# New cost numbers for the list scheduler of a fused attention and two-MLP kernel

## The chip, the core and the metric

One core of a Trainium2 chip runs the whole program. The metric is the device time of one launch in microseconds (us). Engines are named as the profile names them: PE (TensorE matmul) and PEld (its weight load), DVE (VectorE), ACT (ScalarE), POOL (GpSimd) and SP (SyncE, which issues all the DMAs here). Each engine works through its own instruction stream strictly in order; an instruction whose inputs are not there holds up everything behind it on that engine.

## What is computed

```
scores = 0.125 * q @ k^T                      # 4 batches x 8 heads, 576 x 576, head size 64
keep the scores >= the row's 32nd largest      # top_k = 32
a = softmax of the kept ones;  x = a @ v       # x becomes [2304, 512]
h = x @ w_in;  x = (h * cos(h)) @ w_out        # 512 -> 2048 -> 512
P = exp(x @ w_gate), normalised 8 times over rows and columns    # [2304, 8]
out = sum over e of P[:, e] * (relu(x @ w1[e]) @ w2[e])          # 8 experts, 512 -> 1024 -> 512
```

w_in and w_out arrive as 64-bit floats, as pairs of 32-bit words.

## The kernel before

Rows of x are handled in tiles of 128 tokens. An *attention tile* (`att_tile`, L436) is 128 queries of one head against all 576 keys; there are 144 of them. On DVE such a tile is a MAX8 (L459), three rounds of MATCH_REPLACE8 (L464) and MAX8 (L465) that find the 32nd largest score, a mask that multiplies and sums (L466), and a reciprocal (L469). Around these stand score products on PE (L447 and L448, or L451 for the first tiles), copies and exp on ACT (L457, L461), small steps and the normalisation on POOL (L460, L468, L470), transposes on PE (L475), the split of the transposed tile into a high and a low part (L493 on ACT, L494 on DVE) and the products with v (L501, L503).

Nearly all large products are made of three fp32r products of high and low parts (`mm3`, L370). A weight is loaded by DMA into `raw`, ACT copies it to a high part (L345), and POOL or DVE subtracts for the low part (L347).

The program has these stages, which overlap:

- **Head.** The first three attention tiles of all eight heads (`attention_tile`, 24 of the 144 tiles) are done in plain fp32. Beside them `decode` (L315) turns 32 chunks of w_in and w_out into fp32: a DMA of 0.5 MB, a bit operation on DVE (L325), four ACT steps (L326 to L329), a POOL product (L330), a second bit operation on DVE (L331), two more POOL steps (L332, L333) and a store to DRAM. For each of the three tiles follows the first MLP: `moe1_tile_a` (products L629, the cosine gate with L588 and L589 on POOL, L590 and L595 on DVE, transposes L638) and `moe1_tile_b` (products L654, transposes L661, and the split L668/L669 into `x2fh` and `x2fl`). The third L669 completes x2f for the first 384 tokens.
- **Fills.** From then on PE has `fill(e, 0, 3)` (L762) for all eight experts: expert products for these 384 tokens, which need nothing but weights. They stand beside the rest of attention of batch 0 and all of batch 1. Their gates are L758 on ACT and L759 on DVE.
- **The first wide MLP part** (`moe1`, 512 tokens) needs batch 1's attention to be done; its second products are L383, L384 and L387. It yields x2f for four more tiles, whose fills (`fill(e, 3, 4)`) stand beside the attention of batches 2 and 3.
- **Three more MLP parts, the normalisation of P** (`sinkhorn`), and then 32 rounds over the experts for the remaining tokens.

The code writes none of the order by hand. Every instruction is given to a `Plan` with an engine, an estimated cost in ns, what it reads and writes, and a priority by engine and class of work (`PRIORITY`, L28: on PE the first attention goes first, then the first MLP, then attention, then the rest; on DVE the MLP goes first, then decode, then first attention, then attention). `Plan.issue` plays the engines forward in its own estimated time: it takes the engine that is free earliest, lets it take the ready operation of best priority, and adds the estimated cost and a latency. The order in which operations are taken is the order of the emitted program. So an estimate changes no instruction, only the place at which it stands in its engine's stream. Ring buffers (four raw chunks in decode, two `wk`, four score tiles) turn into dependencies in the same way. Inside a plan DMAs share one rate, and a plan counts a PE product double where it takes PE's clock to be low.

Of the kernel before, what the change touches and what calls it, by code (L numbers as in the profile page):

```python
# [12 lines left out]
I32 = mybir.dt.int32  # L13
U32 = mybir.dt.uint32
AF = mybir.ActivationFunctionType
ALU = mybir.AluOpType
# [7 lines left out]
LOWEST = -3.0e38  # L24
# [46 lines left out]
class Plan:  # L71
# [78 lines left out]
    def issue(self):  # L150
# [15 lines left out]
        while len(order) < len(ops):  # L166
            best = None
            for e in engines:
                if now[e]:
                    t = free[e]  # L170
                elif soon[e]:
                    t = max(free[e], soon[e][0][0])
                else:
                    continue
                if best is None or t < best[0]:
                    best = (t, e)
            t, e = best
            while soon[e] and soon[e][0][0] <= t:
                k = heapq.heappop(soon[e])[1]
                heapq.heappush(now[e], (ops[k].prio, k))  # L180
            k = heapq.heappop(now[e])[1]
            op = ops[k]
            cost = op.cost
            if op.func and op.func != func:
                cost, func = cost + 1283.0, op.func
            if e == "PE":
                w = int(t / 3413)
                if w != window:
                    past = busy.get(w - 1, 0.0) / 3413
                    warm = past > 0.95 or (warm and past > 0.5)  # L190
                    window = w
                cost *= 1.0 if warm else 2.0
                a = t
                while a < t + cost:
                    z = min(t + cost, (int(a / 3413) + 1) * 3413.0)
                    busy[int(a / 3413)] = busy.get(int(a / 3413), 0.0) + z - a
                    a = z
            free[e] = op.end = t + cost
            if e == "SP":
                dma_free = max(t + cost + 650.0, dma_free) + op.bytes / 360.0  # L200
                op.end = dma_free + 900.0
            order.append(k)
            for o in op.outs:
                n = ops[o]
                n.ready = max(n.ready, op.end + self.LAT.get((e, n.eng), 130.0))
                n.left -= 1
                if not n.left:
                    heapq.heappush(soon[n.eng], (n.ready, o))
# [3 lines left out]


def mm_ns(n):
    return max(107.0, n / 2.4 + 3.0)


def act_ns(n, psum=False, ap=False):
# [11 lines left out]
def fused_kernel(tc, kq, vv, w_in, w_out, w_gate, w1, w2, out, B=4):  # L230
# [31 lines left out]
    def put(eng, cost, emit, reads=(), writes=(), func=None, nbytes=0):  # L262
        return add(eng, cost, emit, reads, writes, PRIORITY[eng][CLASSES.index(work)], func, nbytes)
# [51 lines left out]
    def decode(src, keep, part):  # L315

        raw, mag, sgn, low = d_raw(), d_mag(), d_sgn(), d_low()  # L320
        dma(lambda: raw.ap, lambda: src.bitcast(I32), 1 << 19, writes=[raw])
        hi = lambda dt: raw.ap.bitcast(dt).rearrange("p (n t) -> p n t", t=2)[:, :, 1]
        lo = lambda: raw.ap.bitcast(U32).rearrange("p (n t) -> p n t", t=2)[:, :, 0]
        magf = lambda: mag.ap.bitcast(F32)
        put("DVE", 335, lambda: V.tensor_scalar(mag.ap, hi(I32), 3, 0x40000000, op0=ALU.logical_shift_left, op1=ALU.bitwise_xor), [raw], [mag])  # L325
        put("ACT", 613, lambda: A_.activation(sgn.ap, hi(F32), AF.Identity, bias=cols.ap[:, 1:2]), [raw, cols], [sgn])  # L326
        put("ACT", 613, lambda: A_.activation(sgn.ap, sgn.ap, AF.Sign, bias=cols.ap[:, 2:3]), [sgn, cols], [sgn])
        put("ACT", 520, lambda: A_.activation(low.ap, lo(), AF.Copy, scale=2.0**-52), [raw], [low])
        put("ACT", 520, lambda: A_.activation(magf(), magf(), AF.Abs), [mag], [mag])  # L329
        put("POOL", 1225, lambda: G_.tensor_tensor(magf(), magf(), sgn.ap, op=ALU.mult), [mag, sgn], [mag])  # L330
        put("DVE", 335, lambda: V.tensor_scalar(sgn.ap.bitcast(I32), mag.ap, -8388608, None, op0=ALU.bitwise_and), [mag], [sgn])  # L331
        put("POOL", 1225, lambda: G_.tensor_tensor(low.ap, low.ap, sgn.ap, op=ALU.mult), [low, sgn], [low])  # L332
        put("POOL", 1225, lambda: G_.tensor_tensor(low.ap, magf(), low.ap, op=ALU.add), [mag, low], [low])  # L333
        dma(keep, lambda: low.ap, 1 << 18, [low], [part])
# [101 lines left out]
    def att_tile(stats, dests, plain=None):  # L436
# [24 lines left out]
        put("ACT", act_ns(S, ap=True), lambda: A_.activation(ex.ap, sc.ap, AF.Exp, scale=0.125, bias=mc(32)), [sc, (m, 32, 33)], [ex], func="exp")  # L461
        for r in range(3):
            src = wk if r else sc
            put("DVE", 669, lambda r=r, src=src: V.match_replace(wk.ap, mc(8 * r, 8), src.ap, LOWEST), [src, (m, 8 * r, 8 * r + 8)], [wk])  # L464
            put("DVE", 669, lambda r=r: V.max(mc(8 * r + 8, 8), wk.ap), [wk], [(m, 8 * r + 8, 8 * r + 16)])  # L465
        put("DVE", 729, lambda: V.scalar_tensor_tensor(ex.ap, sc.ap, mc(31), ex.ap, op0=ALU.is_ge, op1=ALU.mult, accum_out=mc(33)),  # L466
            [sc, ex, (m, 24, 32)], [ex, (m, 33, 34)])
        put("POOL", 162, lambda: G_.tensor_scalar(mc(34), mc(33), 1e-9, 1.0, op0=ALU.add, op1=ALU.mult), [(m, 33, 34)], [(m, 34, 35)])  # L468
        put("DVE", 75, lambda: V.reciprocal(mc(35), mc(34)), [(m, 34, 35)], [(m, 35, 36)])  # L469
# [624 lines left out]
```

## Time and profile before

| what | value |
|---|---|
| three runs, us | 2480.79, 2482.40, 2483.55; median 2482.4 |
| the profiled execution, us | 2480.47; span 2478.7 |
| PE busy | 2364.7 us, 95% |
| DVE busy | 1986.9 us, 80% |
| ACT, POOL busy | 1271.7 us and 1266.6 us, 51% each |
| chain that ended last, by engine | PE 57%, DVE 28%, POOL 6% |
| DMA | 261.37 MB, mean 105 GB/s, 263 GB/s in the busiest of 40 slices |

Busy means that an instruction of the engine was under way; a matmul is pipelined and its end modelled, so that matmuls that start 0.227 us apart are each 0.39 us long and overlap. The chain of waits follows the last instruction back to what released each step. Both PE and DVE stand high, so the stages have to be read apart, which the rows further down do.

### The profile page before, as it was taken

The page shows a single profiled execution, that of the slowest core. Times are in us where ns is not written, and L with a number is a line of the kernel's source. Part 1 is how long each engine was busy: PE and PEld are TensorE (multiplying, and loading weights), DVE is VectorE, ACT ScalarE, POOL GpSimd, SP SyncE. Part 2 cuts the span into 40 slices and gives each one's busy share as a digit, 9 for nine tenths or more (in the row PEclk, how much of TensorE's full clock was granted, in tenths as well). Part 3 has the DMA queues.
Part 4 walks back from the last instruction along what each step waited for, and adds up shares of the span by engine and source line. Part 5 has one row for each costly group of instructions (what it writes and reads, how often), then busy time and mean ns, then how long its engine had stood idle before and what let it go on. Part 6 is the DMA issues. An engine that isn't in the chain of part 4 may idle for free.

```text
span 2478.7 us, 33516 instructions
## 1 busy us (share of the span) xinstructions
PE 2364.7 (95%) x11089; PEld 1905.7 (77%) x11089; DVE 1986.9 (80%) x3651; ACT 1271.7 (51%) x2438; POOL 1266.6 (51%) x1328
## 2 busy tenths in 40 slices
PE   6878999999889999999999999999999999999999
PEld 3434688888667877778878888788888888888887
DVE  8997599999998999999986787776666666666655
ACT  6785566666578666666566776322322222322221
POOL 6886487767577656656520033433443334443330
PEclk9889999999899999999999999999999999999999
DMA  8765654444323333333334333022222221111101
GB/s 263 232 210 186 200 167 144 139 123 151 109 74 97 114 115 115 115 119 97 97 114 123 91 108 104 27 64 81 81 85 81 73 60 35 36 42 43 35 22 47
DMA packets 159501, 261.37 MB, mean 105 GB/s; under 512 B 15008, under 2 KB 60656, under 8 KB 159328
## 3 DMA queue, kind: packets, MB, share of 16 engines
q1 hardware_dynamic: 159328, 259.24, 34.5%
q8 instruction: 87, 1.43, 0.2%
q14 instruction: 86, 0.70, 0.1%
HBM read 227.31 MB, written 31.87 MB: 105 GB/s over the span
## 4 chain that ended last, share of the span: by engine, by line
PE 57%; DVE 28%; POOL 6%; issue 4%; ACT 3%; DMA 1%; SPq 0%; POOLq 0%; ACTq 0%; DVEq 0%
PE y L372 9%; PE y L373 9%; PE y L374 9%; DVE wk L464 7%; DVE m L465 6%; DVE ex L466 4%; PE g L374 2%; PE g L373 2%; PE g L372 2%; DVE m L459 2%; POOL wlo L347 2%; DVE atl L494 1%; PE y L383 1%; PE y L387 1%; PE y L384 1%
## 5 line engine op out<-in xcount | busy, mean ns | idle before, releaser
L347 POOL TENSOR_TENSOR wlo<-raw,whi 128x512 fp32r<-128x512 f32 x336 | 451.7, 1349 | 195.1 <-ACT whi L345 116.3
L465 DVE MAX8 m<-wk 128x8 f32<-128x576 f32 x432 | 318.1, 748 | 1.9
L953 DVE SCALAR_TENSOR_TENSOR acc<-y,P,acc 128x512 f32<-128x512 f32 x308 | 229.2, 748 | 103.5 <-PE y L374 103.2
L345 ACT ACTIVATE whi<-raw 128x512 fp32r<-128x512 f32 x416 | 259.2, 627 | 96.5 <-PE y L374 36.9
L464 DVE MATCH_REPLACE8 wk<-m,wk 128x576 f32<-128x576 f32 x288 | 213.5, 742 | 1.1
L372 PE MATMUL y<-whi,gh 128*128 128x512 f32 x448 | 182.0, 406 | 0.0
L372 PE MATMUL y<-gh,xh 128*128 128x512 f32 x450 | 177.1, 393 | 1.0 <-DVE acc L949 1.0
L374 PE MATMUL y<-whi,gl 128*128 128x512 f32 x448 | 176.5, 394 | 0.0
L373 PE MATMUL y<-gl,xh 128*128 128x512 f32 x450 | 176.5, 392 | 0.0
L374 PE MATMUL y<-gh,xl 128*128 128x512 f32 x450 | 176.2, 392 | 0.0
L373 PE MATMUL y<-wlo,gh 128*128 128x512 f32 x448 | 176.0, 393 | 0.0
L475 PE MATMUL t<-ident,ex 128*128 128x128 f32 (+1 forms) x720 | 136.6, 290 | 39.7 <-POOL ex L470 10.9
L457 ACT ACTIVATE sc<-s 128x288 f32<-128x288 f32 x288 | 117.0, 406 | 95.6 <-DVE ex L466 54.9
L475 PEld LDWEIGHTS t<-ident,ex 128*128 128x128 f32 (+1 forms) x720 | 85.9, 140 | 101.6 <-POOL ex L470 27.8
L466 DVE SCALAR_TENSOR_TENSOR ex<-sc,m,ex 128x576 f32<-128x576 f32 x144 | 152.8, 1061 | 3.6 <-ACT ex L461 1.8
L470 POOL TENSOR_SCALAR ex<-ex,m 128x576 f32<-128x576 f32 x144 | 111.2, 772 | 33.9 <-DVE m L469 33.0
L493 ACT ACTIVATE ath<-t 64x128 fp32r<-64x128 f32 (+3 forms) x272 | 104.5, 396 | 46.2 <-PE t L475 40.0
L461 ACT ACTIVATE ex<-sc,m 128x576 f32<-128x576 f32 x144 | 111.3, 773 | 32.4 <-POOL m L460 31.4
L459 DVE MAX8 m<-sc 128x8 f32<-128x576 f32 x144 | 106.9, 743 | 9.2 <-ACT sc L457 9.1
L464 DVE MATCH_REPLACE8 wk<-m,sc 128x576 f32<-128x576 f32 x144 | 106.7, 741 | 0.0
L372 PEld LDWEIGHTS y<-gh,xh 128*128 128x128 f32 x450 | 85.2, 189 | 20.0 <-DVE acc L949 1.8
L372 PE MATMUL y<-gh,gh 128*128 128x512 f32 x254 | 99.4, 391 | 0.0
(376 smaller groups left out, 7054.6 us busy)
## 6 DMA issues: line engine op xcount, KB each, us to landing
raw<-in_w_dram SPq DMA_DIRECT2D x384, 256.0 KB, 2.6
kq<-in_kq_dram SPq DMA_DIRECT2D x32, 576.0 KB, 4.3
raw<-win_d SPq DMA_DIRECT2D x64, 256.0 KB, 3.0
raw<-wout_d SPq DMA_DIRECT2D x64, 256.0 KB, 2.7
y_d<-st SPq DMA_DIRECT2D x56, 256.0 KB, 3.0
raw<-y_d SPq DMA_DIRECT2D x56, 256.0 KB, 2.7
wp<-win_d SPq DMA_DIRECT2D x24, 512.0 KB, 5.3
wp<-wout_d SPq DMA_DIRECT2D x24, 512.0 KB, 4.4
```

Source lines behind the costliest of these rows:

```text
L345: put("ACT", act_ns(n), lambda: A_.activation(hv(), rv(), AF.Copy), [rb], [hb])
L347: put(e, c, lambda: f.tensor_tensor(lv(), rv(), hv().bitcast(F32), op=ALU.subtract), [rb, hb], [lb])
L372: T_.matmul(o(), ah(), bh(), start=start, stop=False)
L373: T_.matmul(o(), ah(), bl(), start=False, stop=False)
L374: T_.matmul(o(), al(), bh(), start=False, stop=stop)
L457: put("ACT", act_ns(288, psum=True), lambda c=c: A_.activation(sc.ap[:, c], o(), AF.Copy), [ps_s], [(sc, c.start, c.stop)])
L459: put("DVE", 669, lambda: V.max(mc(0, 8), sc.ap), [sc], [(m, 0, 8)])
L464: put("DVE", 669, lambda r=r, src=src: V.match_replace(wk.ap, mc(8 * r, 8), src.ap, LOWEST), [src, (m, 8 * r, 8 * r + 8)], [wk])
L465: put("DVE", 669, lambda r=r: V.max(mc(8 * r + 8, 8), wk.ap), [wk], [(m, 8 * r + 8, 8 * r + 16)])
L466: put("DVE", 729, lambda: V.scalar_tensor_tensor(ex.ap, sc.ap, mc(31), ex.ap, op0=ALU.is_ge, op1=ALU.mult, accum_out=mc(33)), [sc, ex, (m, ...
L475: T_.transpose(pt()[:p, c - c0, :], ex.ap[:, c * 128 : c * 128 + p], ident.ap)
L953: put("DVE", 663, lambda y=y, av=av, pcol=pcol: V.scalar_tensor_tensor(av(), y.ap, pcol(), av(), op0=ALU.mult, op1=ALU.add), [y, P, a], [a])
```

## The change

Six cost numbers are replaced. A product of n columns is estimated at n/2.4 + 13.6 ns instead of n/2.4 + 3; a match-replace at 738 ns instead of 669; the mask at 960 instead of 729; the two bit operations of a decode chunk at 600 each instead of 335; and the DMA rate at 280 bytes per ns instead of 360. Instructions, buffers and priorities are the same.

```diff
-                dma_free = max(t + cost + 650.0, dma_free) + op.bytes / 360.0
+                dma_free = max(t + cost + 650.0, dma_free) + op.bytes / 280.0
...
 def mm_ns(n):
-    return max(107.0, n / 2.4 + 3.0)
+    return max(107.0, n / 2.4 + 13.6)
...
-        put("DVE", 335, lambda: V.tensor_scalar(mag.ap, hi(I32), 3, ...
+        put("DVE", 600, lambda: V.tensor_scalar(mag.ap, hi(I32), 3, ...
...
-            put("DVE", 669, lambda r=r, src=src: V.match_replace(...
+            put("DVE", 738, lambda r=r, src=src: V.match_replace(...
...
-        put("DVE", 729, lambda: V.scalar_tensor_tensor(ex.ap, sc.ap, mc(31), ...
+        put("DVE", 960, lambda: V.scalar_tensor_tensor(ex.ap, sc.ap, mc(31), ...
```

The order changes nearly everywhere up to the end of attention; from the normalisation of P on PE's order is row for row the same. Three places follow. In the names `m`, `wk`, `sc` and `ex` are the buffers of an attention tile, `d_raw`, `d_mag` and `d_sgn` those of decode, `rr` and `hs` those of the gate, `x2fl` the low part of x2f; numbers tell buffers of a ring apart.

The first place is DVE's stream in the head, where the last of the 32 decode chunks ends (L331). Before:

```order
L465 MAX m_127<-wk_134 128x8
L464 MATCH_REPLACE wk_183<-m_169,wk_183 128x576
L464 MATCH_REPLACE wk_134<-m_127,wk_134 128x576
L590 TENSOR_TENSOR rr_703<-rr_703,hs_640 128x1024
L465 MAX m_127<-wk_134 128x8
L465 MAX m_169<-wk_183 128x8
L466 SCALAR_TENSOR_TENSOR ex_223,m_127<-sc_115,m_127,ex_223 128x576
L464 MATCH_REPLACE wk_183<-m_169,wk_183 128x576
L331 TENSOR_SCALAR d_sgn_231<-d_mag_175 128x512
```

And now:

```order
L331 TENSOR_SCALAR d_sgn_193<-d_mag_175 128x512
L465 MAX m_129<-wk_136 128x8
L464 MATCH_REPLACE wk_199<-m_170,wk_199 128x576
L464 MATCH_REPLACE wk_136<-m_129,wk_136 128x576
L465 MAX m_170<-wk_199 128x8
L465 MAX m_129<-wk_136 128x8
L331 TENSOR_SCALAR d_sgn_212<-d_mag_187 128x512
```

The last L331 stood behind 22 first MAX8 (L459), 66 replaces, 65 further MAX8 and 21 masks, with four L590 and six L595; it now stands behind 18, 53, 53 and 16, with two and four. Up to it POOL's stream held 20 normalisations (L470) beside the 32 chunks and now holds 17, counted at the last L333.

The second place is DVE's stream at the end of the head, between the 24th mask and the third L669. Before, the third tile's two gates stand side by side behind tile 25:

```order
L469 RECIPROCAL m_127<-m_127 128x1
L590 TENSOR_TENSOR rr_907<-rr_907,hs_718 128x1024
L595 TENSOR_TENSOR rr_907<-rr_907,hs_718 128x512 x2
L590 TENSOR_TENSOR rr_1152<-rr_1152,hs_1098 128x1024
L595 TENSOR_TENSOR rr_1152<-rr_1152,hs_1098 128x512 x2
L494 TENSOR_TENSOR atl_1612<-t,ath_1604 128x4x128
L459 MAX m_169<-sc_151 128x8
L669 TENSOR_TENSOR x2fl<-y_766,x2fh 128x4x128
```

And now:

```order
L590 TENSOR_TENSOR rr_866<-rr_866,hs_830 128x1024
L465 MAX m_203<-wk_136 128x8
L464 MATCH_REPLACE wk_199<-m_280,sc_206 128x576
L466 SCALAR_TENSOR_TENSOR ex_234,m_203<-sc_177,m_203,ex_234 128x576
L465 MAX m_280<-wk_199 128x8
L469 RECIPROCAL m_203<-m_203 128x1
L464 MATCH_REPLACE wk_199<-m_280,wk_199 128x576
L595 TENSOR_TENSOR rr_866<-rr_866,hs_830 128x512 x2
L465 MAX m_280<-wk_199 128x8
L464 MATCH_REPLACE wk_199<-m_280,wk_199 128x576
L590 TENSOR_TENSOR rr_1161<-rr_1161,hs_1136 128x1024
L494 TENSOR_TENSOR atl_1639<-t,ath_1629 128x4x128
```

The gates are now mixed with tiles 25 to 27, and by the third L669 the stream has passed 29 first MAX8, 87 replaces, 87 further MAX8 and 28 masks, where it had passed 26, 78, 78 and 26.

The third place is PE's stream at the same point, just ahead of the transposes of the third x2 (L661). Before:

```order
L475 MATMUL t<-ident,ex_137 64x128
L447 MATMUL s<-kh_1383,qt_1372 128x288
L448 MATMUL s<-kl_1388,qt_1372 128x288
L447 MATMUL s<-kh_1400,qt_1380 128x288
L448 MATMUL s<-kl_1425,qt_1380 128x288
L661 MATMUL y_754<-ident,st_1449 128x128 x4
```

And now:

```order
L475 MATMUL t<-ident,ex_185 128x128 x4
L447 MATMUL s<-kh_1248,qt_1207 128x288
L448 MATMUL s<-kl_1258,qt_1207 128x288
L447 MATMUL s<-kh_1267,qt_1210 128x288
L448 MATMUL s<-kl_1305,qt_1210 128x288
L661 MATMUL y_797<-ident,st_1397 128x128 x4
```

The rows look alike, but the transposes are those of tile 26 instead of tile 25, and 14 L447 have been passed instead of 6. Ahead of the 24th tile's transposes 38 products of L629 stand instead of 35.

## Rows read from the trace of the kernel before

**Rows 1.** The page's first part: busy us, share of the span, instructions.

```profile
PE 2364.7 (95%) x11089; PEld 1905.7 (77%) x11089; DVE 1986.9 (80%) x3651; ACT 1271.7 (51%) x2438; POOL 1266.6 (51%) x1328
```

**Rows 2.** Busy time by stage: stretch and its length, then engines, clock, DMA.

```profile
core 0: us, PE busy (x) PEld busy (x) DVE busy (x) ACT busy (x) POOL busy (x), PEclk, DMA share, GB/s
0.00:226.00 226.00, 175.73 (x560) 86.91 (x560) 210.67 (x395) 164.32 (x308) 176.17 (x184) 0.91 0.74 229
226.00:285.00 59.00, 54.26 (x188) 27.27 (x188) 20.84 (x40) 23.22 (x41) 15.21 (x21) 0.97 0.59 192
285.00:668.00 383.00, 368.13 (x2052) 324.46 (x2050) 371.14 (x828) 255.89 (x567) 290.72 (x338) 0.99 0.48 144
668.00:1268.00 600.00, 573.45 (x2831) 461.23 (x2830) 581.18 (x1203) 386.81 (x772) 377.36 (x444) 0.99 0.36 104
1612.00:2478.00 866.00, 861.92 (x3924) 727.26 (x3922) 550.57 (x779) 231.53 (x405) 324.54 (x281) 1.00 0.18 56
```

**Rows 3.** Timeline of DVE, 236 to 286: start, us, instruction, idle before it.

```profile
245.63 1.22 DVE L590 TENSOR_TENSOR rr<-rr,hs 128x1024 f32<-128x1024 f32 x1 [5.46 <-POOL rr L589]
...
284.00 0.69 DVE L669 TENSOR_TENSOR x2fl<-y,x2fh 128x512 fp32r<-128x512 f32 x1 [8.42 <-ACT x2fh L668]
```

**Rows 4.** Waits of PE between 620 and 700: total us, times, longest.

```profile
PE s L447 <- ACT sc L457: 7.1, 7, 2.6
```

**Rows 5.** Timeline of PE at 1800: products of 512 columns in a row.

```profile
1799.70 0.39 PE L373 MATMUL y<-gl,xh 128*128 128x512 f32 x1
...
1801.97 0.39 PE L374 MATMUL y<-gh,xl 128*128 128x512 f32 x1
```

**Rows 6.** Groups by line over the whole span: busy, mean ns, idle before.

```profile
L466 DVE SCALAR_TENSOR_TENSOR ex<-sc,m,ex 128x576 f32<-128x576 f32 x144 | 152.8, 1061 | 3.6 <-ACT ex L461 1.8
L470 POOL TENSOR_SCALAR ex<-ex,m 128x576 f32<-128x576 f32 x144 | 111.2, 772 | 33.9 <-DVE m L469 33.0
L331 DVE TENSOR_SCALAR d_sgn<-d_mag 128x512 int32<-128x512 int32 x32 | 26.9, 840 | 2.1 <-POOL d_mag L330 2.0
L325 DVE TENSOR_SCALAR d_mag<-d_raw 128x512 int32<-128x512 int32 x32 | 24.1, 753 | 2.2 <-POOL d_low L333 1.2 <-DMA d_raw<-in_w_in_dram 1.0
```

**Rows 7.** Timeline of DVE at 655, steps back to back; at 667 tile 74's mask.

```profile
655.75 0.09 DVE L464 MATCH_VALUE_LOAD wk<-m,wk 128x8 f32 x1
655.82 0.74 DVE L464 MATCH_REPLACE8 wk<-m,wk 128x576 f32<-128x576 f32 x1
656.48 0.15 DVE L469 RECIPROCAL m<-m 128x1 f32<-128x1 f32 x1
656.55 0.74 DVE L459 MAX8 m<-sc 128x8 f32<-128x576 f32 x1
657.21 0.74 DVE L465 MAX8 m<-wk 128x8 f32<-128x576 f32 x1
...
667.12 0.80 DVE L466 SCALAR_TENSOR_TENSOR ex<-sc,m,ex 128x576 f32<-128x576 f32 x1
```

**Rows 8.** Groups by line on POOL from 0 to 226: the three decode steps.

```profile
L332 POOL TENSOR_TENSOR d_low<-d_low,d_sgn 128x512 f32<-128x512 f32 x32 | 45.8, 1431 | 10.2 <-DVE d_sgn L331 9.6
L333 POOL TENSOR_TENSOR d_low<-d_mag,d_low 128x512 f32<-128x512 f32 x32 | 44.1, 1379 | 1.4
L330 POOL TENSOR_TENSOR d_mag<-d_mag,d_sgn 128x512 f32<-128x512 f32 x32 | 43.5, 1368 | 4.6 <-ACT d_mag L329 4.5
```

**Rows 9.** Timeline of PE from 262 to 286: fp32 products of the third tile.

```profile
270.44 11.37 PE L654 MATMUL y<-wp,gT 128*128 128x512 f32 x26
```

**Rows 10.** Timeline of DVE at 165: the same bit operation twice.

```profile
165.20 0.41 DVE L331 TENSOR_SCALAR d_sgn<-d_mag 128x512 int32<-128x512 int32 x1
166.21 1.04 DVE L331 TENSOR_SCALAR d_sgn<-d_mag 128x512 int32<-128x512 int32 x1
```

**Rows 11.** Timeline of POOL at the same time.

```profile
165.69 1.27 POOL L332 TENSOR_TENSOR d_low<-d_low,d_sgn 128x512 f32<-128x512 f32 x1 [0.72 <-DVE d_sgn L331]
```

More of the change, by code (lines that the diff above doesn't have):

```diff
@@ L324, in decode @@
         magf = lambda: mag.ap.bitcast(F32)
-        put("DVE", 335, lambda: V.tensor_scalar(mag.ap, hi(I32), 3, 0x40000000, op0=ALU.logical_shift_left, op1=ALU.bitwise_xor), [raw], [mag])
+        put("DVE", 600, lambda: V.tensor_scalar(mag.ap, hi(I32), 3, 0x40000000, op0=ALU.logical_shift_left, op1=ALU.bitwise_xor), [raw], [mag])
         put("ACT", 613, lambda: A_.activation(sgn.ap, hi(F32), AF.Identity, bias=cols.ap[:, 1:2]), [raw, cols], [sgn])
@@ L330, in decode @@
         put("POOL", 1225, lambda: G_.tensor_tensor(magf(), magf(), sgn.ap, op=ALU.mult), [mag, sgn], [mag])
-        put("DVE", 335, lambda: V.tensor_scalar(sgn.ap.bitcast(I32), mag.ap, -8388608, None, op0=ALU.bitwise_and), [mag], [sgn])
+        put("DVE", 600, lambda: V.tensor_scalar(sgn.ap.bitcast(I32), mag.ap, -8388608, None, op0=ALU.bitwise_and), [mag], [sgn])
         put("POOL", 1225, lambda: G_.tensor_tensor(low.ap, low.ap, sgn.ap, op=ALU.mult), [low, sgn], [low])
@@ L463, in att_tile @@
             src = wk if r else sc
-            put("DVE", 669, lambda r=r, src=src: V.match_replace(wk.ap, mc(8 * r, 8), src.ap, LOWEST), [src, (m, 8 * r, 8 * r + 8)], [wk])
+            put("DVE", 738, lambda r=r, src=src: V.match_replace(wk.ap, mc(8 * r, 8), src.ap, LOWEST), [src, (m, 8 * r, 8 * r + 8)], [wk])
             put("DVE", 669, lambda r=r: V.max(mc(8 * r + 8, 8), wk.ap), [wk], [(m, 8 * r + 8, 8 * r + 16)])
-        put("DVE", 729, lambda: V.scalar_tensor_tensor(ex.ap, sc.ap, mc(31), ex.ap, op0=ALU.is_ge, op1=ALU.mult, accum_out=mc(33)),
+        put("DVE", 960, lambda: V.scalar_tensor_tensor(ex.ap, sc.ap, mc(31), ex.ap, op0=ALU.is_ge, op1=ALU.mult, accum_out=mc(33)),
             [sc, ex, (m, 24, 32)], [ex, (m, 33, 34)])
```

## The prediction

> **What bounds the kernel now.** I read the busy shares first. PE is under way for 95% of the span and DVE for 80% [rows 1], so no single engine's total tells what a new order is worth, and the next view is the table by stage [rows 2]. It falls into four kinds of stretch.
>
> From 0 to 226 DVE is busy for 210.7 us and idle for 15.3, PE is at 175.7. DVE sets the pace there: 24 attention tiles and 32 decode chunks. From 226 to 285 the picture turns over. DVE works for 20.8 of 59 us, PE for 54.3: the third tile's first MLP runs on PE, and DVE waits for its gate and its x2 [rows 3]. At 284 the third L669 gives the fills free. From 285 to 668 DVE is busy for 371.1 of 383 us and idle for 12. PE reads 368.1, but its products overlap in that count, and at the end of the stretch it stands waiting for scores whose copy the attention tiles hold back [rows 4]: the fills have run out before batch 1's attention has. So DVE ends last here too. From 668 to 1268, where the last attention tile ends, DVE is busy for 581.2 of 600. Behind that PE alone sets the pace: 861.9 of the last 866 us.
>
> The end is therefore the time at which the last attention tile leaves DVE, and the PE work that stands behind it. That first time is DVE's work plus DVE's idle time, and 38 of the 84 us of that idle time lie between 226 and 285.
>
> **The numbers themselves.** The new estimate of a product fits: ten products of 512 columns start 2.27 us apart [rows 5], 0.227 each, and 512/2.4 + 13.6 is 227 ns; it was estimated at 216. A replace with its value load takes 0.73 us from start to start [rows 7], the estimate is now 738 ns. The mask's mean is 1.061 us [rows 6], against 960 now and 729 before. The bit operations take 0.753 and 0.840 on average [rows 6], against 600 and 335. No instruction is added or removed, so what counts is the order. I cost it by counting, in each stream, what stands before the points on which the stages end.
>
> **Part 1: decode moves ahead in the head.** Take per MAX8 0.66 us and per replace 0.73 [rows 7], 1.06 per mask and 0.75 + 0.84 per chunk [rows 6], and leave the gates out. Up to the last L331 DVE had 87 x 0.66 + 66 x 0.73 + 21 x 1.06 + 32 x 1.59 = 179 us; now 71 x 0.66 + 53 x 0.73 + 16 x 1.06 + 51 = 154 us. POOL has 32 x (1.368 + 1.431 + 1.379) = 134 us in either case [rows 8], and 20 or 17 normalisations of 0.77 [rows 6], so 149 or 147 us. The cushion between the two streams falls from 30 us to 7. POOL will sometimes not be ready, and DVE, in order, will stand at an L331. At the least this costs nothing, since so far DVE idled only 15.3 us in 226, most of it before its first tile. At the most POOL keeps the idle share that it has now, 50 of 226 us [rows 2]: 147/0.78 is 188 us, and the last L331 comes 34 us later than 154. That is far too much, as POOL's idle time lay behind a DVE that did attention instead; half of it, 17, I take as the upper bound. The row that I hold nearest is DVE's own idle time, so I take +5.
>
> Where a 512-wide bit operation starts with POOL free it takes 0.41 us; one that starts at 166.21, while L332 holds from 165.69 for 1.27, takes 1.04 and ends just behind it [rows 10, 11]. So a part of the "measured" 0.75 and 0.84 is waiting for POOL, and depends on the order that the estimate makes. The Trainium skill says this as a rule (SBUF — State Buffer, "Who interferes with whom"): DVE in a 2-port mode and GpSimd exclude each other on a shared port pair for a whole instruction; the trace agrees. By that rule alone the right estimate would be the free duration plus a wait, not 600, and a denser decode would lengthen these operations. In rows: if all 64 met the 1.04 of row 166.21 instead of the mean 0.80, the head would gain 15 us; if none met POOL, it would lose 25. I take no change for the centre, since POOL's work is the same and lies beside DVE's all the time, and carry the 15 as a rival.
>
> **Part 2: the third x2.** Ahead of the 24th mask, which ends the third tile, DVE now has 2 MAX8, 2 replaces, a reciprocal and an L669 more: 1.3 + 1.5 + 0.15 + 0.7 = +3.6 us. Behind it PE has three products of L629 less to do, each two passes of 11.37/26 = 0.44 us [rows 9]: -2.6. The gates now stand behind tiles 25 and 26 on DVE; PE covers this with the second tile's L654 products, which stand between the gates' transposes. With +5 from part 1 the third L669 comes 6 us later, at 291; bounds 0 and 18.
>
> **Part 3: what DVE has done by then.** The stream has passed 12 MAX8, 9 replaces, 2 masks, 2 reciprocals and an L494 more: 12 x 0.66 + 9 x 0.73 + 2 x 1.06 + 0.3 + 0.7 = 17.6 us. It fits into the 38 idle us from 226 to 285 (5.46 us before L590 and 8.42 before the last L669 are two of its pieces [rows 3]), because the scores of these tiles are now placed early on PE. From the third L669 to the mask of tile 74, which ends the stretch at 668 [rows 7], DVE then has 371 - 17.6, and one MAX8 and one small addition more (+1.1): 355 us. Its idle time was 12; with PE, whose work there is the same to one group of three products, now nearer to DVE's, I take 15. That is 370 instead of 383: -13. The bounds are -16.5 (no more idle time than before) and 0 (PE sets the pace).
>
> **Part 4: the rest.** Between tile 74 and the last mask DVE has 3 L347, 2 L494 and an L759 less and the pieces above already behind it: about -5 us. But PE has 21 products of 512 columns fewer ahead of the last tile's transposes, 21 x 0.227 = 4.8 us, and they come behind it, where PE alone counts. Sum 0, bounds 3 to either side. From the normalisation of P on the PE order is the same.
>
> **Sum.** +6 - 13 + 0 = -7 us on the profiled execution's 2480.5, so 2473.5. The median of the three runs, 2482.4, is 1.9 above that execution, which makes **2475 us**.
>
> **Rivals.**
>
> *The early gain is eaten in the head.* POOL and the port hold up the denser decode: the third L669 comes 17 us later instead of 6. For it: a cushion of 7 us over 150, and operations that wait for each other anyway. Against it: after the last chunk POOL has little to do, and tiles 17 to 24 run without it. Then +17 - 13 = +4, 2486 us: no change that can be told. To the same side belongs the case that the order hardly matters, with each part near nothing: 2482 us.
>
> *PE sets the pace from 285 to 668.* Then the 17.6 us of DVE's work done early turn into idle time of DVE, part 3 is worth nothing, and the later third L669 stays: +6, 2488 us. It decides if the stretch from the third L669 to the mask of tile 74 is longer than 380 us. For it: 368 of 383 us read as busy on PE. Against it: the waits of PE at the end of the stretch [rows 4], and DVE's idle time of only 12 us in 383.
>
> *The head is late by 25 us.* All of the above bounds together, 15 for the port and 10 for POOL; then +25 - 13 = +12, 2494 us. It decides if the third L669 falls behind 303.
>
> **How the numbers follow.** The forecast, 2475, has 0.53; the first rival, with the order that hardly matters, 0.27 at 2482 to 2486; the second 0.12 at 2488; the third 0.08 at 2494. The forecast's own spread is 0 to 12 for the third L669, -16.5 to -9 for the stretch and 3 for the rest: 2463 to 2482. The range from 2462 to 2491 leaves out the third rival and a little of the second on one side and a few hundredths below. A measurement of this kernel can tell about 0.2%, 5 us, from no change; faster than 2477.4 is 0.53, within 0.2% 0.27, slower 0.20.
>
> **What will show it.** In the profile of the changed kernel the last L331 of the head should end near 170 to 180 us, the third L669 near 291, and DVE should be idle between the 24th mask and the third L669 for about 20 us instead of 38. The mask of tile 74 should end near 661 and the last mask near 1256 to 1260. PE should wait less for scores between 620 and 700. If the third L669 is behind 303, part 1 was wrong; if it is near 291 and tile 74 still ends at 668, part 3 was; if both fit and the end does not, part 4. The forecast is wrong as a whole if DVE's idle time up to the last mask, 84 us now, has not fallen.

## The result and the profile after

The changed kernel takes 2496.5 us (four runs, 2495.7 to 2497.9), the kernel before 2482.4 beside it: a ratio of 1.0058, 95% interval 1.0040 to 1.0075. It is slower by 14 us, where 7 us less were forecast; the time lies above the range, next to the rival of the late head (2494). The profiled spans are 2494.1 and 2478.7 us.

Two rows of the page after, the first as in [rows 1], the second the chain that ended last by engine:

```profile
PE 2378.7 (95%) x11089; PEld 1903.4 (76%) x11089; DVE 2019.0 (81%) x3651; ACT 1268.5 (51%) x2434; POOL 1266.7 (51%) x1328
...
PE 63%; DVE 19%; POOL 7%; ACT 6%; issue 3%; DMA 1%; POOLq 0%; SPq 0%; ACTq 0%; DVEq 0%
```

Most totals hardly differ from [rows 1]; DVE is busy for 32 us more, 26 of them behind the last mask, where PE sets the pace. The stages differ more. The same table as [rows 2], of the kernel after. Its first boundary is that of [rows 2], the next ones are its own third L669 (303), mask of tile 74 (679.5, cut at 675) and last mask (1275):

```profile
0.00:226.00 226.00, 175.62 (x503) 86.37 (x504) 196.87 (x359) 160.54 (x297) 177.36 (x180) 0.83 0.71 220
226.00:303.00 77.00, 70.68 (x263) 36.88 (x262) 53.45 (x112) 34.45 (x68) 24.67 (x37) 0.96 0.60 189
303.00:675.00 372.00, 360.62 (x2012) 314.69 (x2010) 357.38 (x783) 251.36 (x552) 281.68 (x325) 1.00 0.48 143
675.00:1275.00 600.00, 573.69 (x2823) 455.20 (x2823) 581.75 (x1203) 378.23 (x762) 381.94 (x443) 0.99 0.36 104
...
1612.00:2494.00 882.00, 877.18 (x3989) 739.23 (x3987) 577.83 (x796) 235.25 (x410) 321.35 (x284) 1.00 0.19 55
```

In the first 226 us DVE was busy for 210.7 and is now for 196.9, with PE at a lower granted clock (0.83 for 0.91, means over stretches at its two levels, 1.2 and 2.4 GHz). Measured from point to point, in us (the 24th mask ends the third tile's attention):

| from | to | before | after | difference | forecast |
|---|---|---|---|---|---|
| start | 24th mask | 226.0 | 245.4 | +19.4 | +8.6 |
| 24th mask | third L669 | 58.7 | 57.4 | -1.3 | -2.6 |
| third L669 | mask of tile 74 | 383.2 | 376.7 | -6.5 | -13 |
| mask of tile 74 | last mask | 599.9 | 595.6 | -4.3 | -5 |
| last mask | end | 1210.9 | 1219.0 | +8.1 | +5 |

The middle rows go in the direction that was forecast. The losses are in the head and, 8 us, in the tail. DVE's idle time tells what kind of loss the first is: up to the 24th mask it was 15.3 us [rows 2] and is 29.3. Who is waited for there stands in the waits of DVE from 20 to 250 us, here of the kernel after (waiting line, awaited line, total us, times, longest):

```profile
DVE m L469 <- POOL m L468: 8.3, 5, 2.8
DVE d_sgn L331 <- POOL d_mag L330: 7.9, 9, 2.4
```

The same view of the kernel before:

```profile
DVE m L469 <- POOL m L468: 2.6, 2, 2.3
DVE d_sgn L331 <- POOL d_mag L330: 2.0, 3, 0.9
```

The 2.6 us at L469 stand behind the 24th mask there. Up to the 24th mask these two waits thus grew from 2 to 16 us, which is all of the 14.0. One of the nine at L331, in the timeline of DVE after (start, us, instruction, idle before it):

```profile
158.66 0.41 DVE L325 TENSOR_SCALAR d_mag<-d_raw 128x512 int32<-128x512 int32 x1
158.99 0.75 DVE L465 MAX8 m<-wk 128x8 f32<-128x576 f32 x1
159.66 0.82 DVE L325 TENSOR_SCALAR d_mag<-d_raw 128x512 int32<-128x512 int32 x1
160.40 1.82 DVE L466 SCALAR_TENSOR_TENSOR ex<-sc,m,ex 128x576 f32<-128x576 f32 x1
...
162.23 0.74 DVE L464 MATCH_REPLACE8 wk<-m,wk 128x576 f32<-128x576 f32 x1
162.89 0.74 DVE L459 MAX8 m<-sc 128x8 f32<-128x576 f32 x1
163.55 0.74 DVE L465 MAX8 m<-wk 128x8 f32<-128x576 f32 x1
166.64 0.43 DVE L331 TENSOR_SCALAR d_sgn<-d_mag 128x512 int32<-128x512 int32 x1 [2.35 <-POOL d_mag L330]
```

What lies between, on ACT:

```profile
159.74 1.28 ACT L461 ACT_TABLE_LOAD   x1
...
162.68 0.75 ACT L326 ACTIVATE d_sgn<-d_raw,cols 128x512 f32<-128x512 f32 x1
...
164.65 0.62 ACT L329 ACTIVATE d_mag<-d_mag 128x512 f32<-128x512 f32 x1
```

and on POOL:

```profile
165.35 1.26 POOL L330 TENSOR_TENSOR d_mag<-d_mag,d_sgn 128x512 f32<-128x512 f32 x1 [3.75 <-ACT d_mag L329]
```

The chunks pass each engine in the same order, and the L331 at 166.64, the 27th, belongs to the L325 at 158.66, the 27th too; the one at 159.66 is the next chunk's. So the first bit operation ends at 159.07, and the chunk's way through ACT and POOL ends at 166.61, 7.5 us later, since ACT is still with an exp, its table and a copy and begins the chunk at 162.68. The new order has put 5.2 us of other work between the two bit operations (up to 164.29), and DVE, in order, stands for the rest. POOL is not short of time here: it stood idle for 3.75 us itself.

### The profile page after: what moved, and what is told of

It reads as the page before. It is cut to its first block, busy times and chain, and to the rows that moved or that the text cites. A ratio compares the mean times of both kernels' runs of the same rounds, so it can differ in the third digit from the quotient of the medians.

```text
span 2494.1 us, 33473 instructions
## 1 busy us (share of the span) xinstructions
PE 2378.7 (95%) x11089; PEld 1903.4 (76%) x11089; DVE 2019.0 (81%) x3651; ACT 1268.5 (51%) x2434; POOL 1266.7 (51%) x1328
## 3 DMA queue, kind: packets, MB, share of 16 engines
q8 instruction: 87, 1.43, 0.2%
## 4 chain that ended last, share of the span: by engine, by line
PE 63%; DVE 19%; POOL 7%; ACT 6%; issue 3%; DMA 1%; POOLq 0%; SPq 0%; ACTq 0%; DVEq 0%
PE y L372 9%; PE y L373 9%; PE y L374 9%; DVE wk L464 4%; DVE m L465 3%; DVE ex L466 3%; PE g L374 2%; PE g L372 2%; PE g L373 2%; POOL wlo L347 2%; PE t L475 2%; PE h L374 1%; PE h L373 1%; PE h L372 1%; PE y L383 1%
## 5 line engine op out<-in xcount | busy, mean ns | idle before, releaser
L347 POOL TENSOR_TENSOR wlo<-raw,whi 128x512 fp32r<-128x512 f32 x336 | 456.2, 1361 | 236.1 <-ACT whi L345 180.3
L466 DVE SCALAR_TENSOR_TENSOR ex<-sc,m,ex 128x576 f32<-128x576 f32 x144 | 167.0, 1160 | 2.8 <-ACT ex L461 1.8
L470 POOL TENSOR_SCALAR ex<-ex,m 128x576 f32<-128x576 f32 x144 | 111.0, 771 | 24.9 <-DVE m L469 24.1
L459 DVE MAX8 m<-sc 128x8 f32<-128x576 f32 x144 | 107.1, 743 | 10.6 <-ACT sc L457 10.6
```

What stands on the lines that cost most here:

```text
L347: put(e, c, lambda: f.tensor_tensor(lv(), rv(), hv().bitcast(F32), op=ALU.subtract), [rb, hb], [lb])
L466: put("DVE", 960, lambda: V.scalar_tensor_tensor(ex.ap, sc.ap, mc(31), ex.ap, op0=ALU.is_ge, op1=ALU.mult, accum_out=mc(33)), [sc, ex, (m, ...
```

## Experiments

### One family of estimates at a time

The first theory: decode's two DVE estimates rose alone, while its POOL steps stay at 1225 ns (they take 1.37 to 1.43 us [rows 8]) and its ACT steps at 520 and 613, so that the plan thinks a chunk ready too early. Then the bit operations carry the loss, and measured estimates for all of decode's steps remove it.

**e1_bits_back**, from the kernel after:

```diff
-        put("DVE", 600, lambda: V.tensor_scalar(mag.ap, ...
+        put("DVE", 335, lambda: V.tensor_scalar(mag.ap, ...
...
-        put("DVE", 600, lambda: V.tensor_scalar(sgn.ap.bitcast(I32), ...
+        put("DVE", 335, lambda: V.tensor_scalar(sgn.ap.bitcast(I32), ...
```

> The new numbers but for the two bit operations, which are back at 335 ns. Theory (POOL has no cushion in the head): in the changed kernel DVE's work ahead of an L331 is only 5 to 8 us more than POOL's ahead of its L330, where it grew from 9 to 27 us before; here it grows from 8 to 23 again, so the third L669 should be near 287 (285 before, 303.5 in the changed kernel), DVE's wait for POOL at L331 and L469 near 5 us instead of 16, and the time near 2482. Rival A (the estimates of replace and mask do it, by the place at which the mask meets POOL): the time stays at 2494 and the mean of the mask between the head and the end of attention stays at 1.14 us. Rival B (any other order of the head loses, by chance): third L669 near 300.

Measured: 2494.7 us, ratio 1.0058 (1.0043 to 1.0073). The third L669 is back at 284.6, but the stretch behind it takes 397.8 us instead of 376.7, and the end is as late as after.

**e2_bits_alone**, from the kernel before: the same two lines, 335 to 600.

> The kernel before with only the two bit operations at 600 ns. The last L331 moves ahead of the 19th tile (from the 21st), DVE's lead over POOL stays at 8 to 11 us instead of growing to 27. Theory: half of the loss in the head, third L669 at 292 to 297, time 2484 to 2492. Rival A: no loss, 2482. The order has no tiles 27 and 28 ahead of the third L669 here, so nothing is given back in the next stage.

Measured: 2485.6 us, 1.0019 (1.0010 to 1.0028), third L669 at 283.9. So the bit operations are neither sufficient nor necessary for the loss: on the numbers of before they cost 5 us, and without them the other four numbers cost 14. e1 was expected near the kernel before; its head was, its end was not. e2 also answers for PE's clock, which had fallen in the head of the kernel after. Up to e2's 24th mask:

```profile
0.00:229.00 229.00, 175.69 (x557) 88.35 (x558) 215.46 (x395) 165.12 (x308) 178.94 (x188) 0.82 0.72 227
```

The granted clock is as low as there, and DVE is idle for 13.5 us instead of 29.3: the lower clock alone does not make DVE wait.

**e3_pool_act_measured**, from the kernel after:

```diff
-        put("ACT", 613, ...)    # L326, L327
+        put("ACT", 735, ...)
...
-        put("ACT", 520, ...)    # L328, L329
+        put("ACT", 645, ...)
...
-        put("POOL", 1225, ...)  # L330, L332, L333
+        put("POOL", 1395, ...)
```

> The changed kernel, and the estimates of decode's three POOL steps and four ACT steps set to measured ones as well (POOL 1225 to 1395 ns, ACT 613 to 735 and 520 to 645). All estimates of the change stay. The last L331 goes back behind the 20th tile, DVE's lead over POOL grows from 8 to 19 us, and 29 masks stand ahead of the third L669 as a gain. Theory: third L669 near 290, DVE's waits for POOL in the head 5 us, time 2475 to 2484. Rival A: 2494, since replace, mask and bit operations keep their new numbers. Rival B: anywhere between 2482 and 2500.

Measured: 2475.7 us, 0.9983 (0.9973 to 0.9992): 19 us better than after by the profiled spans (2475.4 and 2494.1), with the third L669 at 286.3 and the stretch at 373.6. The rest of decode's estimates, at what the trace shows, give back the head and keep the gain behind it.

**e4_replace_mask_alone**, from the kernel before:

```diff
-            put("DVE", 669, lambda r=r, src=src: V.match_replace(...
+            put("DVE", 738, lambda r=r, src=src: V.match_replace(...
...
-        put("DVE", 729, lambda: V.scalar_tensor_tensor(ex.ap, ...
+        put("DVE", 960, lambda: V.scalar_tensor_tensor(ex.ap, ...
```

> The kernel before with only the replace at 738 and the mask at 960 ns. DVE's lead over POOL in the head grows from 9 to 21 us, 28 masks stand ahead of the third L669, and 22 us more of PE's work stand ahead of the last tile's transposes. Theory: no loss in the head (third L669 285 to 291), time 2470 to 2482. Rival A: slower, 2490 or more, with a mask mean of 1.14 us.

Measured: 2512.4 us, 1.0129 (1.0114 to 1.0144), a miss. The order holds more of DVE's work ahead of the last mask (1215.8 us busy up to it, 1183.6 in the kernel before) and 22 us more of PE's products ahead of the last tile; the last mask ends at 1311.6. By stage (us, then PE, PEld, DVE, ACT, POOL busy, the granted clock):

```profile
1190.00:1299.00 109.00, 103.41 (x512) 84.67 (x510) 106.23 (x215) 74.91 (x142) 47.01 (x61) 1.00 0.33 103
1299.00:1333.00 34.00, 14.94 (x44) 10.80 (x45) 16.71 (x39) 5.68 (x14) 2.96 (x7) 0.50 0.05 13
```

For 34 us before and behind the last mask every engine is idle for half the time or more, and PE is at the lower of its two clocks (0.50, which is 1.2 GHz). That PE, with 22 us more of its products already done, had too little left to do there fits, but was not tested.

**e5_product_replace_mask**, the change without the bit operations and without the DMA rate; against e1 it differs in one line:

```diff
-                dma_free = max(t + cost + 650.0, dma_free) + op.bytes / 280.0
+                dma_free = max(t + cost + 650.0, dma_free) + op.bytes / 360.0
```

> The change without the bit operations and without the DMA rate. It differs from the first run (bit operations back) in the DMA rate alone. Account of four terms (third L669; DVE work left from there to tile 74 and on; the mask's waits for POOL; PE work behind the last mask): DVE's lead over POOL in the head grows from 9 to 20 us, so the third L669 is near 287 to 292; 28 masks stand ahead of it where the first run had 25, so the stretch from there to tile 74 takes 365 to 372 us instead of 398; 2470 to 2480 in all. Rival A (the mask's and the replace's estimates make the order slow): 2490 or more, as with these two alone.

Measured: 2487.5 us, 1.0030 (1.0020 to 1.0041), later than expected. Against e1 it shows what DVE's early work is worth. Up to the third L669 and to the mask of tile 74, first e1:

```profile
0.00:285.00 285.00, 236.78 (x742) 117.97 (x743) 221.24 (x419) 184.73 (x344) 188.35 (x200) 0.92 0.70 222
285.00:682.00 397.00, 374.44 (x2053) 324.20 (x2051) 382.89 (x837) 261.04 (x571) 293.55 (x342) 0.98 0.46 139
```

and e5:

```profile
0.00:298.00 298.00, 243.66 (x770) 122.53 (x770) 257.06 (x480) 198.00 (x370) 204.68 (x222) 0.86 0.70 220
298.00:663.00 365.00, 354.27 (x1983) 308.44 (x1984) 352.96 (x776) 246.61 (x542) 275.77 (x318) 1.00 0.46 140
```

In e5 DVE has done 36 us more when the third L669 ends; that comes 14 us later, and the stretch behind it is 33 us shorter. A later third L669 is therefore no loss by itself; DVE's idle time ahead of it is. What makes e5 slower than the kernel before is the work behind its last mask, 1220.9 us instead of 1210.9; the last mask itself ends 3.5 us earlier.

**e8_pool_act_without_bits**: e3 with the two bit operations at 335.

> As the third run (POOL and ACT steps of decode at measured values), but with the bit operations back at 335 ns. DVE's lead over POOL grows to 38 us, 28 masks stand ahead of the third L669, PE work behind the last mask is as in the changed kernel. Four terms: third L669 284 to 290, tile 74 near 658, end 2468 to 2480. If the bit operations' estimate had a worth of its own beyond the cushion, this is slower than the third run (2476).

Measured: 2484.6 us, 1.0015 (1.0006 to 1.0024), slower than expected. Raising the bit operations from 335 to 600 thus costs 5 us on the numbers of before (e2), nothing that can be told on those of e1 (1.0058 there and in the kernel after), and gains 9 on those of e8 (to e3). The estimates do not add up one by one.

### Is POOL short of time?

The prediction had costed the head by a cushion between two streams, 30 us before and 7 now. If POOL's time were short, taking one of its three steps away would free the kernel after and do little before.

**e6_after_pool_relieved** (from after) and **e7_before_pool_relieved** (from before) leave out the product of the low part with the sign, so that the low parts of w_in and w_out lack their sign:

```diff
-        put("POOL", 1225, lambda: G_.tensor_tensor(low.ap, low.ap, sgn.ap, op=ALU.mult), [low, sgn], [low])
+        put("POOL", 1225, lambda: None, [low, sgn], [low])
```

> The changed kernel in its own order, with one of decode's three POOL steps left out when instructions are emitted (the product of the low part with the sign, L332, 32 x 1.43 us); the low parts of w_in and w_out then lack their sign. If POOL has no cushion in the head, the third L669 comes 10 to 18 us earlier (285 to 293 instead of 303) and the end with it, 2478 to 2487. If ACT, the DMAs or PE's low clock hold the head up, the third L669 stays at 300 or later and the time above 2491.

> The control: the kernel before in its own order, with the same POOL step (L332) left out; the low parts lack their sign here too. POOL had a cushion there, so the third L669 moves by less than 5 us and the time is 2475 to 2483. If relief of POOL is worth the same here as in the changed kernel, POOL's cushion is not what the change took away.

Measured: 2476.6 us, 0.9989 (0.9980 to 0.9999), and 2466.3 us, 0.9944 (0.9929 to 0.9959). The third L669 moves by -20.0 us in the first, where 10 to 18 were expected, and by -14.9 in the second, where under 5 were. And what got shorter is not the waits. Up to the 24th mask of e6:

```profile
0.00:226.00 226.00, 183.91 (x597) 93.41 (x597) 193.29 (x404) 167.75 (x317) 137.43 (x158) 0.86 0.75 237
```

and the waits of DVE from 20 to 250 in e6:

```profile
DVE d_sgn L331 <- POOL d_mag L330: 12.0, 11, 4.0
DVE m L469 <- POOL m L468: 6.8, 5, 2.8
```

DVE's idle time is 32.7 us against 29.3 after; its busy time fell from 216.2 to 193.3, as its own instructions are shorter: L331 takes 0.696 us on average, 0.956 after, and the mask up to 300 us 0.882 instead of 1.242. With a third of POOL's decode work gone the two waits are 18.8 us, against 16.2. Three quarters of the relief come in the old order as well, with its cushion of 30 us. The theory of the short POOL falls.

### The distance between dependent steps

The theory in its place: an instruction of DVE that needs a result which went out over ACT and POOL has to stand far enough behind the one that sent it. Summed from the order with the durations of [rows 6, 7], the DVE work between a chunk's two bit operations, and the two waits of 20 to 250 us:

| kernel | work between, mean us | pairs under 6 us, of 32 | wait at L331, us | at L469, us |
|---|---|---|---|---|
| before | 14.8 | none | 2.0 | 2.6 |
| after | 7.7 | 8 (7 under 5) | 7.9 | 8.3 |
| e1 | 10.2 | 4 | 6.7 | 4.5 |
| e3 | 13.3 | 1 | 1.2 | 3.7 |
| e5 | 13.8 | none | 1.5 | 2.2 |
| e9 | 9.6 | 1 (5.8) | 0.4 | 1.2 |
| e10 | 10.0 | none (least 6.8) | 0.1 | none |

The wait at L331 goes with the short pairs and not with the mean: e9 has less work between than e1 and hardly waits. Nor is there one distance that is always enough: in the kernel after the way from the first bit operation to the end of L330 takes 3.1 to 17.0 us, and of the seven pairs under 5 us three wait, for 4.4 of the 7.9 us, and four do not. Between a mask and its reciprocal 2.1 us of other work stand before, 1.4 after, 2.2 in e1, 1.6 in e5, 4.2 in e9 and 5.9 in e10; the two latency runs have the longest distances and the least waits, but among the others the mean distance alone does not order the waits at L469.

**e9_latency_2500** and **e10_latency_4000** leave the six new numbers as they are and tell the plan that a result of POOL reaches DVE later, which keeps such steps apart in the order:

```diff
-        ("POOL", "ACT"): 69.0, ("POOL", "DVE"): 70.0, ...
+        ("POOL", "ACT"): 69.0, ("POOL", "DVE"): 2500.0, ...
```

(4000.0 in e10.)

> The changed kernel with one more estimate altered: the plan's latency from POOL to DVE is 2500 ns instead of 70. Relieving POOL moved the third L669 by 20 us in the changed kernel and by 15 in the kernel before, and DVE's idle time up to the 24th mask did not fall (32.7 us): so POOL's throughput is not what the change took away. New theory: what it took away is distance. Between a chunk's first and second bit operation DVE has 14.8 us of other work in the order before and 7.7 in the changed one (7 of 32 under 5 us), and between a mask and its reciprocal 2.1 and 1.4; the round trip over ACT and POOL does not fit, and DVE stands. Here decode stays early (last L331 behind the 17th tile), the distances are 9.6 (none under 5.8) and 4.2 us. Theory: DVE's waits for POOL at L331 and L469 fall from 16 us to under 5, the 24th mask ends at 232 to 236 instead of 245, the end near 2482. If the early decode itself holds the head up (ports, ACT, DMAs), the 24th mask stays at 242 or later.

> As the run before it, with 4000 ns. Distances 10.0 us (none under 6.8) and 5.9; last L331 behind the 20th tile; 259 us of DVE work ahead of the third L669, the most of all orders, where the changed kernel has 249. 5 us less of PE's work stand ahead of the last tile's transposes. Theory: waits for POOL at L331 and L469 under 3 us, third L669 285 to 292, the stretch to tile 74 near 362, end 2472 to 2482.

Measured: e9 2482.0 us, 1.0006 (0.9997 to 1.0015); e10 2471.2 us, 0.9965 (0.9952 to 0.9978), faster than both kernels. Decode still runs early in e9 (the last L331 at 181.9; 192.3 after, 209.5 before), so it is not the early decode that costs. The waits of DVE from 20 to 250 in e9:

```profile
DVE rr L595 <- ACT rr L592: 4.4, 2, 2.7
DVE x2fl L669 <- ACT x2fh L668: 3.0, 1, 3.0
DVE rr L590 <- POOL rr L589: 2.9, 1, 2.9
DVE m L469 <- POOL m L468: 1.2, 1, 1.2
DVE d_sgn L331 <- POOL d_mag L330: 0.4, 1, 0.4
```

The two waits fell from 16.2 to 1.6 us. The 24th mask came 7.6 us earlier, less than expected, as the waits of the gate and of x2's split, the first three rows, took part of the room: 10.3 us, where the kernel after has 2.8. The end came 14 us earlier, as much as the change had lost, but this is not the head's alone. The latency holds for the whole plan, and the wait of the reciprocal for POOL, up to the last mask, is in the kernels before and after and in e9:

```profile
DVE m L469 <- POOL m L468: 9.4, 15, 2.3
DVE m L469 <- POOL m L468: 21.9, 28, 2.8
DVE m L469 <- POOL m L468: 1.2, 1, 1.2
```

Between the mask of tile 74 and the last mask it takes 6.1 us in the kernel after and nothing in e9, and there e9 is 7 us shorter. So the pair of mask and reciprocal costs more in all than decode's pair, and most of it behind the head. What each of e9's other changes of place is worth was not taken apart.

In e10 the third L669 is at 301.2, almost where it is after and not where it was expected:

```profile
236.00:301.00 65.00, 57.70 (x192) 29.90 (x190) 44.70 (x93) 29.24 (x56) 25.87 (x35) 0.92 0.58 190
301.00:655.00 354.00, 346.49 (x1957) 306.00 (x1958) 344.59 (x763) 242.18 (x532) 275.81 (x312) 1.00 0.47 141
```

But DVE is busy for 44.7 of the 65 us ahead of it (20.8 of 59 before [rows 2]) and has done 259.9 us of work by then, 10 more than after; the stretch behind takes 354.1 us.

### Does the longer mask carry the loss?

Up to the last mask the masks take 14.2 us longer in sum than before (1.160 us each against 1.061 [rows 6]), which is as much as the whole loss, and tempting. A mask that starts under a POOL L347 ends behind it, as here in the kernel after; with POOL free it takes 0.81:

```profile
1107.12 1.29 POOL L347 TENSOR_TENSOR wlo<-raw,whi 128x512 fp32r<-128x512 f32 x1
1107.60 1.42 DVE L466 SCALAR_TENSOR_TENSOR ex<-sc,m,ex 128x576 f32<-128x576 f32 x1
```

The Trainium skill has this as a rule (SBUF — State Buffer, "Who interferes with whom"): a DVE instruction with two SBUF inputs contends with a GpSimd instruction that reads SBUF, one with a single input outside the 2-port modes does not. So the mask was given one input, in after (**e11_after_mask_one_input**) and in before (**e12_before_mask_one_input**). It compares and sums, and leaves out the product with the exponentials, so that attention's weights are no longer those of the softmax:

```diff
-  V.scalar_tensor_tensor(ex.ap, sc.ap, mc(31), ex.ap, op0=ALU.is_ge, op1=ALU.mult, accum_out=mc(33)),
+  V.tensor_scalar(ex.ap, sc.ap, mc(31), 1.0, op0=ALU.is_ge, op1=ALU.add, accum_out=mc(33)),
```

> The changed kernel in its own order, with the mask as an operation of one SBUF input: it compares and sums, and leaves out the product with the exponentials, so attention's weights are zeros and ones. Behind the third L669 a mask that starts while POOL is free takes 0.81 us, and one that starts under POOL's L347 1.24 to 1.34; the sum of what masks take beyond 0.81 is 38.5 us there, in the kernel before 25.4. If that is waiting for POOL, every mask now takes 0.8 us and the stretch from the third L669 to the last mask shortens by 30 to 38 us. If a long mask has another reason, its mean stays above 1.1.

> The control: the kernel before in its own order with the same mask of one input (attention's weights zeros and ones). The stretch from the third L669 to the last mask, 983 us, shortens by 20 to 25. The difference of the changed kernel's stretch to this one's, -10.8 us with the full mask, goes to -20 to -26 if the masks' waits ate 13 us of part 3's gain.

Measured: 2461.8 us, 0.9926 (0.9912 to 0.9941), and 2445.4 us, 0.9860 (0.9844 to 0.9877). The groups of the mask from 300 to 1280, after:

```profile
L466 DVE SCALAR_TENSOR_TENSOR ex<-sc,m,ex 128x576 f32<-128x576 f32 x116 | 132.2, 1140 | 1.0
```

and e11:

```profile
L466 DVE TENSOR_SCALAR_CACHE_REDUCE ex<-sc,m 128x576 f32<-128x576 f32 x116 | 93.3, 805 | 1.0
```

The trace agrees with the rule: 0.805 us on average with one input, 1.140 with two. But the difference between the orders stays: the spans of e11 and e12 are 2460.3 and 2443.2, 17.1 us apart; those of the kernels after and before are 15.4 apart. DVE's busy time up to the last mask, first after:

```profile
0.00:1275.10 1275.10, 1180.72 (x5595) 893.25 (x5596) 1189.55 (x2457) 824.57 (x1675) 865.65 (x984) 0.97 0.47 141
```

then e11:

```profile
0.00:1241.80 1241.80, 1164.14 (x5592) 899.21 (x5593) 1142.98 (x2456) 821.97 (x1675) 843.27 (x984) 0.96 0.48 145
```

and e12:

```profile
0.00:1233.40 1233.40, 1163.25 (x5622) 907.34 (x5623) 1146.61 (x2463) 827.80 (x1686) 838.31 (x984) 0.97 0.48 147
```

With short masks DVE idles for 98.8 us in the order of after and for 86.8 in that of before. What the mask gives back DVE partly spends waiting, and the loss of the change is still there. Of the stretch from the third L669 to the last mask the gain of the new order rose from 10.8 to 13.5 us, where over 20 were expected: the longer masks explain some 3 us.

## Why the prediction was wrong

Each kernel's end can be written as DVE's work up to the last mask, DVE's idle time up to it, and what follows, in us:

| kernel | DVE work | DVE idle | last mask | behind it | span |
|---|---|---|---|---|---|
| before | 1183.6 | 84.2 | 1267.8 | 1210.9 | 2478.7 |
| after | 1189.5 | 85.5 | 1275.1 | 1219.0 | 2494.1 |
| e1 | 1178.9 | 95.3 | 1274.2 | 1217.7 | 2491.9 |
| e2 | 1182.2 | 77.2 | 1259.4 | 1223.1 | 2482.5 |
| e3 | 1188.4 | 69.3 | 1257.6 | 1217.8 | 2475.4 |
| e4 | 1215.8 | 95.8 | 1311.6 | 1198.7 | 2510.3 |
| e5 | 1192.3 | 72.0 | 1264.3 | 1220.9 | 2485.2 |
| e8 | 1181.8 | 82.6 | 1264.4 | 1218.2 | 2482.6 |
| e9 | 1186.9 | 75.2 | 1262.1 | 1217.8 | 2479.9 |
| e10 | 1187.0 | 59.9 | 1246.9 | 1222.7 | 2469.6 |

The prediction said that it is wrong as a whole if the idle time, 84 us, has not fallen. It has not: between the 24th mask and the third L669 it fell by 14.8 us, and ahead of the 24th mask it rose by 14.0.

- **What bounds the kernel** held: in all of these kernels the last mask and the PE work behind it set the end, and between the kernels the idle time moves more than the work does, but for e4, whose order holds 32 us more work ahead of the last mask.
- **Part 1 failed, and with it the sum.** Its +5 was chosen between 0 and 17; with the +3.6 of order the 24th mask should have come 8.6 us later and came 19.4 later: order and busy time +5.5, idle time +14.0. The last L331 of the head ended at 192.3, where 170 to 180 was forecast. The step that failed is the cushion. It compared the sums of two streams up to the last L331, that is, whether POOL has time enough, and e6 shows that this was not the question. What showed in its place are waits of single pairs of dependent steps that stand too close, 7.9 us at L331 and 8.3 at L469 where there had been 2.0 and none; the order showed these pairs, and they were not looked at. That DVE, in order, stands at an L331 was right; the size was not, and half of the wait, at L469, was not thought of. The row held nearest, DVE's idle time of before, was taken in the old order, whose pairs stood 14.8 us apart.
- **The port** in the head was left at no change, with 15 us for a rival. L331 and L325 together grew from 51.0 to 53.3 us: right.
- **Part 2** held: the piece between the 24th mask and the third L669 fell by 1.3, 2.6 forecast. DVE idles there for 23.1 us (52.4 up to the third L669 less 29.3), "about 20 instead of 38" was forecast.
- **Part 3** had the right mechanism: by the third L669 DVE has done 250.3 us instead of 231.5, 17.6 more forecast, and e5 and e10 show that such work comes off the stretch behind. The size failed: -13 against -6.5. DVE's work there was to be 355 and is 361.9, of which the longer masks (1.143 us for 1.029 each, 46 of them) are 5; its idle time, 14.9, was the 15 forecast. PE's wait for scores fell as foretold, from 7.1 [rows 4] to 3.3 us between 620 and 700.
- **Part 4**: -5 up to the last mask was -4.3. The tail, +4.8 by 21 products, was +8.1 (the 21 are those ahead of the last tile's fifth transpose; ahead of its first it is 27). Behind the last mask PE is busy for 4.7 us more, so the 4.8 are there (rows below). The rest is PE's idle time, 21.0 us for 17.5; 2.4 us of it are waits for DVE at L821, in the normalisation of P (4.2 for 1.8 us). Why DVE came later there is not settled.
- **The rivals.** The third L669 came 18.1 us later, at 302.8. That is next to the 17 of the first rival (2486 us) and just ahead of the 303 that decided for the late head (25 us later, 2494 us). That the measured time lies near 2494 is in part luck: the late head was 7 us too much, the -13 behind it was -6.5, and part 4, at nothing there, cost 3.8. Both rivals also had the wrong parts, POOL's time and the port, where it was waiting. The bound of 17 for part 1 had been halved on no row, and the idle time came close to it. PE did not set the pace behind the third L669: that stretch became shorter (376.7 us, and over 380 would have decided for it).

The rows of part 4, behind the last mask, before and after:

```profile
1267.90:2478.70 1210.80, 1193.28 (x5467) 1005.88 (x5465) 803.18 (x1189) 441.56 (x753) 407.18 (x344) 1.00 0.22 66
1275.10:2494.10 1219.00, 1197.95 (x5495) 1010.17 (x5494) 829.44 (x1195) 443.98 (x759) 401.07 (x344) 1.00 0.23 67
```

Why the order of e4 or e8 comes out as it does is not settled; each holds several changes of place, and no run takes them apart. The same holds for the size of e9's and e10's gain.

## What to carry to other kernels

When an order changes, look at every pair of steps between which a result leaves the engine and returns, and compare the work that stands between them with the time of the way; sums over the streams hide it. An estimate of one engine in a list scheduler moves the work of all the others, so it is safer to mend the whole chain of a step at once and to measure the order that comes out. Here four or six of them, each nearer to the trace than it was, cost 14 us, and with decode's other steps set to the trace as well the kernel was 5 us faster than before. Where the plan has a latency between engines, raising it keeps such pairs apart: 4000 instead of 70 ns from POOL to DVE, on the changed numbers, gave 0.35% against the kernel before, and 2500 gave nothing against it. It is the best of the ten orders here, and no run says which latency gives it.

## What was not expected of the hardware

The mask's second input costs more than its place in the profile suggests: with one input the kernel before is 35.5 us shorter, with 0.804 us for 1.061 each (37 us in sum), and nearly all of it reaches the end. In the order of the kernel after 34 of 51 us do. A POOL step taken away made DVE faster rather than POOL readier: 32 steps of 1.43 us fewer, and DVE's busy time up to the 24th mask fell by 22.9 us in one order and by 18.6 in the other.
